# Which engine makes the lo parts of the decoded weights: GpSimd or VectorE

## The chip, the cores and the metric

The kernel runs on one core of one Trainium2 chip. The metric is the device time of one execution in microseconds (us), lower is better; several executions are timed and the median is used. One execution is profiled, and the profile and its trace are what is read here. PE is TensorE (PEld its weight loads), DVE VectorE, ACT ScalarE, POOL GpSimd, SP the engine that issues all DMAs.

## What is computed

The reference chains three blocks on a batch of 4 with 576 positions and 512 channels (8 heads of 64). Cut to what matters:

```python
out_d  = softmax_attention(q_mean4, k_mean4, v_mean4)         # 144 positions
x      = repeat4(out_d) + local_attention(q, k, v, |i-j|<4)   # per head
gate   = sigmoid(causal_conv5(x, conv_w))
x      = (gate * (x @ w_val)) @ w_out
h      = relu(x.T @ w_tok1) @ w_tok2
u      = x + h.T
return u + relu(u @ w_ch1) @ w_ch2
```

All arrays are float32 for the reference. The kernel gets the weights as the bits of 64-bit floats and has to turn them into float32 itself.

## The kernel before

Every large product is made of three TensorE passes (`mm3`, lines 214 to 218): each operand is held as a hi part (rounded to the type fp32r) and a lo part (what the rounding left), and hi*hi, hi*lo and lo*hi are added up.

**Decoding a weight.** `decode` (lines 126 to 151) takes a piece of at most 128 x 256 weights. SP loads the 64-bit words into a tile with the tag `w64` (three buffers). DVE puts the bits together in three steps, lines 135, 136 and 138, into a tile `wa` (three buffers). Then `split` (lines 141 to 143) makes hi on ACT (line 142) and lo on POOL (line 143). A `wa` buffer comes free when its lo is made, so the first step (L135) of the piece three places later waits for that lo.

There are 75 such pieces: 8 of `w_val` (tiles val_hi, val_lo), 8 of `w_out` (out_hi, out_lo), 5 of `w_tok1` (tok_hi, tok_lo), 6 of `w_tok2` (tok_hl), 24 of `w_ch1` (w_hl) and 24 of `w_ch2` (ch). The `w_ch1` tiles are also stored to DRAM as soon as both lo parts are there (line 187, on SP's queue) for use with the later batches.

**Stages.** First (up to about 80 us) the attention of batch 0 runs with the decoding of `w_val` and `w_out` and of the first pieces of `w_tok1`; PE has little to do and is kept going by matmuls on zeros (`busy`, L108). Then a mix of generators runs: `p1(b)` (val product, out product, token products) and `c1(b)` (first channel product) on PE in an order written out by hand (`manual_schedule`), with the attention of batches 1 to 3 and the decoding set between them. The last stage is `c2`, the second channel product.

**Order on the other engines.** DVE, ACT, POOL and SP work in order, each through its own list. A planner makes the lists by priority and by its own estimate of when inputs are ready; nothing is re-ordered while the kernel runs. From the second stage on, `split` is put off until the next piece is decoded (`pending`, `flush`), and its ACT instruction is put behind the ACT copy that empties the latest PE product (`behind_pace`, `paced`).

**What else DVE and POOL do.** DVE makes the convolution (`gate_sb`, L388 and L393), the maxima and reciprocals of the softmax (L251, L261), the sum of the two attentions (`x_f`, L383), `y` (L509) and lo parts that come from PSUM (`x_hl` L533, `r_hl` L574). POOL makes the products by the reciprocal (`e_l`, `e_d`, L262), the sums of v (`v_sb` L291, `vd` L292) and the lo parts of activations (L471).

Of the kernel before, what the change touches and what calls it, by code (L numbers as in the profile page):

```python
# [9 lines left out]
F32 = mybir.dt.float32  # L10
# [5 lines left out]
ALU = mybir.AluOpType  # L16
# [58 lines left out]
def kernel(ctx, tc, qk, vw, v4, w_val, conv_w, w_out, w_tok1, w_tok2, w_ch1, w_ch2, out):  # L75
    nc = tc.nc
# [5 lines left out]
    def T(p, shape, dt, tag, bufs, name=None):  # L82
        return p.tile(shape, dt, tag=tag, bufs=bufs, name=name or tag)
# [37 lines left out]
    def flush():  # L121
        while pending:
            with behind_pace():
                pending.pop(0)()

    def decode(src, n, rows, hi, lo, full=None, shape=None, keep=0):
        x = T(sb, [128, n, 2], I32, "w64", NWD, name="w64")[0:rows]
        a = T(sb, [128, n], I32, "wa", NWD, name="wa")[0:rows]
        if shape is None:
            nc.sync.dma_start(out=x, in_=src.bitcast(I32).rearrange("p (n t) -> p n t", t=2))  # L130
        else:
            nc.sync.dma_start(out=x.rearrange("p (k n) t -> p k n t", k=shape[0]),
                              in_=src.bitcast(I32).rearrange("p k (n t) -> p k n t", t=2))
        low, high = x[:, :, 0], x[:, :, 1]
        nc.vector.tensor_scalar(a, high, 3, 0x3FFFFFF8, ALU.logical_shift_left, ALU.bitwise_and)  # L135
        nc.vector.scalar_tensor_tensor(out=a, in0=high, scalar=-0x40000000, in1=a,  # L136
                                       op0=ALU.bitwise_and, op1=ALU.bitwise_or)
        nc.vector.scalar_tensor_tensor(out=a if full is None else full.bitcast(I32), in0=low, scalar=29, in1=a,
                                       op0=ALU.logical_shift_right, op1=ALU.bitwise_or)

        def split():
            nc.scalar.activation(out=hi, in_=a.bitcast(F32), func=AF.Copy)
            nc.gpsimd.tensor_tensor(out=lo, in0=a.bitcast(F32), in1=hi.bitcast(F32), op=ALU.subtract)

        if full is None:
            if paced[0]:
                if not keep:
                    flush()
                pending.append(split)
            else:  # L150
                split()

    def load_w(key, pieces, tag, bufs, parts=None):

        for j, group in enumerate(pieces):
            n = group[0][1].shape[1]
            hi, lo = parts or [T(sb, [128, len(group), n], F32R, tag, bufs, name=f"{key}{j}_{p}") for p in ("hi", "lo")]
            for i, (rows, src) in enumerate(group):
                for c in range(0, n, WB):
                    e = min(n, c + WB)  # L160
                    decode(src[:, c:e], e - c, rows, hi[0:rows, i, c:e], lo[0:rows, i, c:e])
                wt[key].append((hi[:, i, :], lo[:, i, :]))
                yield
# [16 lines left out]
    def ch1_new(f):  # L180

        t = T(sb, [128, 2, DM], F32R, "w1", NW1R, name="w1_hl")
        src = w_ch1[:, f * 128:f * 128 + 128].rearrange("(k p) c -> p k c", p=128)
        for c in range(0, KC, 2):
            decode(src[:, c:c + 2], 256, 128, *[t[:, i, c * 128:c * 128 + 256] for i in range(2)], shape=(2, 128),
                   keep=c)
        pending.append(lambda: nc.sync.dma_start(out=w1_dr[:, f], in_=t.bitcast(F32)))
        return t
# [6 lines left out]
    def ch2_new():  # L195

        slots = [("wt1", 2)] * 2 + [("w2", NW)] * 8 + [("wt2", 1)]
        f = 0
        for tag, bufs in slots:
            if tag == "w2":  # L200
                pairs = [[T(sb, [128, 1, DM], F32R, tag, bufs, name=f"ch2_{f}_{p}")[:, 0] for p in range(2)]]
            else:
                n = 1 if tag == "wt1" else 2
                t = T(sb, [128, n, 2, DM], F32R, tag, bufs, name=f"ch2_{f}")
                pairs = [[t[:, i, p] for p in range(2)] for i in range(n)]
            for hl in pairs:
                wt["ch2", f] = hl
                for c in range(0, DM, 256):
                    decode(w_ch2[f * 128:f * 128 + 128, c:c + 256], 256, 128, *[t[:, c:c + 256] for t in hl])
                    yield  # L210
                f += 1
        flush()
# [485 lines left out]
    a = [attention(b) for b in range(B)]  # L698
# [7 lines left out]
    side += [(a[b], NA, *A_AT[b]) for b in range(1, B)]  # L706
    last = c2()
    side += [(ch2_new(), 24, *W2_AT), (last, 1, C2_AT, C2_AT + 1)]
    with tc.manual_schedule(engines={mybir.EngineType.PE}):
        mix(first_products(), side)  # L710
# [44 lines left out]
```

## Time and profile before

| | us |
|---|---|
| median of three runs | 664.81 (663.02 to 667.72) |
| the profiled execution, its own time | 669.0 |
| span of the profiled execution, first to last instruction | 667.2 |

| engine | busy us in the span | share |
|---|---|---|
| PE | 626.9 | 94% |
| DVE | 335.7 | 50% |
| ACT | 300.5 | 45% |
| POOL | 209.2 | 31% |

How to read the views: "busy" counts the time in which an engine executes; an instruction's duration includes time in which it is held up at its operands. "Idle before" an instruction is the time in which its engine did nothing, with the instruction that ended the idleness behind an arrow. Times of single instructions are from the start of the span. PEclk is the TensorE clock that was granted, as a share of full speed.

### The profile page before, as it was taken

What the parts mean: (1) busy time and instruction counts of PE and PEld (TensorE: products, weight loads), DVE (VectorE), ACT (ScalarE), POOL (GpSimd) and SP (SyncE); (2) the same over time, 40 slices, a digit from 0 to 9 for tenths busy, and PEclk for the clock granted to TensorE, in tenths of its full rate; (3) what the DMA queues carried; (4) which work ended last, traced back from release to release, by engine and by line L of the source; (5) the groups of instructions that cost most, each with busy time, mean ns of one, the idle gap of its engine ahead of it and who ended that gap; (6) DMA issues with size and microseconds to landing.
All of it is one profiled execution on the core that took longest, in us unless ns stands there. A gap on an engine that the chain in (4) does not pass through costs nothing.

```text
span 667.2 us, 12820 instructions
## 1 busy us (share of the span) xinstructions
PE 626.9 (94%) x4911; PEld 534.6 (80%) x4911; DVE 335.7 (50%) x630; ACT 300.5 (45%) x1032; POOL 209.2 (31%) x242
## 2 busy tenths in 40 slices
PE   8898698888889999999999999999998999999997
PEld 4344487776778988999898999999897888888887
DVE  3679947788795476443343434106626242423232
ACT  1766546564557645637655635324433222222221
POOL 5564613448446432623331323304523000000000
PEclk8899797888989999999999999999998999999999
DMA  7653202565776346784332486566998345454221
GB/s 251 217 160 102 74 21 73 155 209 160 247 231 175 100 165 172 225 244 143 93 87 70 135 240 208 163 196 198 298 299 277 94 139 179 141 175 126 80 69 42
DMA packets 53900, 107.23 MB, mean 161 GB/s; under 512 B 5776, under 2 KB 21392, under 8 KB 53840
## 3 DMA queue, kind: packets, MB, share of 16 engines
q1 hardware_dynamic: 53840, 106.42, 51.8%
q8 instruction: 38, 0.62, 0.4%
q14 instruction: 22, 0.18, 0.1%
HBM read 76.52 MB, written 29.88 MB: 159 GB/s over the span
## 4 chain that ended last, share of the span: by engine, by line
PE 71%; DVE 12%; ACT 6%; DMA 5%; issue 2%; POOL 2%; SPq 1%; DVEq 0%; ACTq 0%; POOLq 0%
PE p_o L216 7%; PE p_o L217 7%; PE p_o L218 7%; PE g_ps L216 6%; PE g_ps L217 6%; PE g_ps L218 6%; DMA w<-in_w_ch_dram 3%; PE sc_l L348 3%; DVE wa L135 3%; DVE wa L136 2%; PE p_x L216 2%; DVE gate_sb L393 2%; PE p_val L217 2%; PE p_val L218 2%; PE p_x L217 2%
## 5 line engine op out<-in xcount | busy, mean ns | idle before, releaser
L216 PE MATMUL g_ps<-u_hl,w_hl 128*128 128x288 f32 x384 | 118.2, 308 | 0.3 <-DVE x_hl L533 0.3
L217 PE MATMUL g_ps<-u_hl,w_hl 128*128 128x288 f32 x384 | 115.5, 301 | 2.5 <-POOL u_hl L471 2.3
L218 PE MATMUL g_ps<-u_hl,w_hl 128*128 128x288 f32 x384 | 114.5, 298 | 0.0
L216 PE MATMUL p_o<-g_hl,ch 128*128 128x512 f32 (+1 forms) x240 | 89.5, 373 | 1.7 <-ACT r_sb L617 1.7
L217 PE MATMUL p_o<-g_hl,ch 128*128 128x512 f32 (+1 forms) x240 | 89.0, 371 | 0.0
L218 PE MATMUL p_o<-g_hl,ch 128*128 128x512 f32 (+1 forms) x240 | 89.0, 371 | 0.0
L471 DVE TENSOR_TENSOR g_hl<-r_back,g_hl 128x512 fp32r<-128x512 f32 (+1 forms) x60 | 38.1, 639 | 92.8 <-ACT g_hl L470 91.2
L470 ACT ACTIVATE g_hl<-r_back 128x512 fp32r<-128x512 f32 (+1 forms) x60 | 35.2, 589 | 108.8 <-PE p_o L218 106.4
L217 PEld LDWEIGHTS g_ps<-u_hl,w_hl 128*128 128x128 f32 x384 | 73.6, 192 | 4.1 <-POOL u_hl L471 4.1
L216 PEld LDWEIGHTS g_ps<-u_hl,w_hl 128*128 128x128 f32 x384 | 73.3, 191 | 4.2 <-issue 2.1
L218 PEld LDWEIGHTS g_ps<-u_hl,w_hl 128*128 128x128 f32 x384 | 73.6, 192 | 0.0
L617 ACT ACTIVATE r_sb<-g_ps 128x288 f32<-128x288 f32 x96 | 38.8, 407 | 61.4 <-PE g_ps L218 52.5
L393 DVE SCALAR_TENSOR_TENSOR gate_sb<-x_f,cw,gate_sb 128x575 f32<-128x575 f32 (+5 forms) x68 | 63.4, 938 | 1.4 <-ACT gate_sb L390 0.5
L216 PEld LDWEIGHTS p_o<-g_hl,ch 128*128 128x128 f32 x240 | 45.6, 190 | 10.1 <-ACT r_sb L617 2.4
L135 DVE TENSOR_SCALAR wa<-w 128x256 int32<-128x256 int32 (+2 forms) x76 | 33.8, 452 | 39.3 <-DMA w<-in_w_ch_dram 21.8
L217 PEld LDWEIGHTS p_o<-g_hl,ch 128*128 128x128 f32 x240 | 45.7, 190 | 7.8
L218 PEld LDWEIGHTS p_o<-g_hl,ch 128*128 128x128 f32 x240 | 45.6, 190 | 7.9
L257 ACT ACTIVATE e_l<-sc_l,mx 128x64 f32<-128x64 f32 x160 | 48.0, 331 | 0.6
L216 PE MATMUL p_val<-x_hl,val_hi 128*128 128x288 f32 x128 | 40.5, 316 | 3.8 <-DVE y L509 2.6
L471 POOL TENSOR_TENSOR x_hl<-x_f,x_hl 128x288 fp32r<-128x288 f32 x32 | 28.1, 889 | 49.4 <-ACT x_hl L470 49.2
L216 PE MATMUL p_x<-y_hl,out_hi 128*128 128x288 f32 x128 | 40.3, 315 | 2.5 <-ACT u_sb L522 1.7
L136 DVE SCALAR_TENSOR_TENSOR wa<-w,wa 128x256 int32<-128x256 int32 (+2 forms) x76 | 41.6, 556 | 1.3
(108 smaller groups left out, 1343.9 us busy)
## 6 DMA issues: line engine op xcount, KB each, us to landing
w_hl<-w_dr SPq DMA_DIRECT2D x36, 512.0 KB
r_dr<-r_sb SPq DMA_DIRECT2D x48, 288.0 KB
w<-in_w_ch_dram SPq DMA_DIRECT2D x48, 256.0 KB
r_back<-r_dr SPq DMA_DIRECT2D x48, 256.0 KB
qk_sb<-in_qk_dram SPq DMA_DIRECT2D x16, 589.0 KB
w_dr<-w_hl SPq DMA_DIRECT2D x12, 512.0 KB
v_sb<-in_vw_dram SPq DMA_DIRECT2D x16, 320.0 KB
v_sb<-in_v_dram SPq DMA_DIRECT2D x16, 288.0 KB
```

Of the source, the lines that this page charges most:

```text
L135: nc.vector.tensor_scalar(a, high, 3, 0x3FFFFFF8, ALU.logical_shift_left, ALU.bitwise_and)
L136: nc.vector.scalar_tensor_tensor(out=a, in0=high, scalar=-0x40000000, in1=a, op0=ALU.bitwise_and, op1=ALU.bitwise_or)
L216: nc.tensor.matmul(out_ap, lhsT=lh, rhs=rh, start=first, stop=False)
L217: nc.tensor.matmul(out_ap, lhsT=lh, rhs=rl, start=False, stop=False)
L218: nc.tensor.matmul(out_ap, lhsT=ll, rhs=rh, start=False, stop=last)
L257: nc.scalar.activation(out=e[:, o, :], in_=p[:, c, :], func=AF.Exp, scale=scale, bias=mx[:, o:o + 1], accum_out=sm[:, o:o + 1])
L348: nc.tensor.matmul(p[r0:r0 + 64, c, :], lhsT=qk[r0:r0 + 64, 0, 3 + o:3 + o + WIN], rhs=qk[r0:r0 + 64, 1, o:o + WIN], start=False, stop=(c ...
L393: nc.vector.scalar_tensor_tensor(out=g[:, t0:s1], in0=x[:, t0 - sh:s1 - sh], scalar=cw[:, hp, k:k + 1], in1=g[:, t0:s1], op0=ALU.mult, op1 ...
L470: nc.scalar.activation(out=hi_ap, in_=src_ap, func=AF.Copy)
L471: lo_eng.tensor_tensor(out=lo_ap, in0=src_ap, in1=hi_ap.bitcast(F32), op=ALU.subtract)
L617: paced[0] = nc.scalar.activation(out=r[:, hv(hs)], in_=p[:, 0:HS], func=AF.Relu)
```

## The change

`decode` gets a parameter for the engine that makes the lo part. Its default is DVE; only the 24 pieces of `w_ch2` keep POOL. So 51 subtractions (8 + 8 + 5 + 6 + 24) go from POOL's list to DVE's. Nothing else differs.

```diff
-    def decode(src, n, rows, hi, lo, full=None, shape=None, keep=0):
+    def decode(src, n, rows, hi, lo, full=None, shape=None, keep=0, lo_eng=nc.vector):
...
         def split():
             nc.scalar.activation(out=hi, in_=a.bitcast(F32), func=AF.Copy)
-            nc.gpsimd.tensor_tensor(out=lo, in0=a.bitcast(F32), in1=hi.bitcast(F32), op=ALU.subtract)
+            lo_eng.tensor_tensor(out=lo, in0=a.bitcast(F32), in1=hi.bitcast(F32), op=ALU.subtract)
...
-                    decode(w_ch2[f * 128:f * 128 + 128, c:c + 256], 256, 128, *[t[:, c:c + 256] for t in hl])
+                    decode(w_ch2[f * 128:f * 128 + 128, c:c + 256], 256, 128, *[t[:, c:c + 256] for t in hl],
+                           lo_eng=nc.gpsimd)
```

## Rows read from the trace of the kernel before

**Rows 1.** Busy time by stage: PE, PEld, DVE, ACT, POOL (instructions), granted clock, DMA share, GB/s.

```profile
0.00:80.00 80.00, 68.99 (x556) 34.68 (x556) 56.54 (x113) 44.96 (x191) 46.45 (x57) 0.91 0.54 168
80.00:260.00 180.00, 159.76 (x1466) 141.18 (x1467) 124.21 (x241) 99.99 (x389) 82.77 (x90) 0.91 0.49 154
260.00:667.20 407.20, 398.18 (x2891) 358.73 (x2889) 154.91 (x278) 155.56 (x454) 79.98 (x95) 0.99 0.54 163
```

**Rows 2.** Longest waits of PE: instruction, who ended it, us, times, longest.

```profile
PE o_d L329 <- DVE x_f L383: 3.2, 1, 3.2
PE pt_d L315 <- DVE x_f L383: 3.0, 1, 3.0
...
PE p_h L216 <- DVE r_hl L574: 2.5, 1, 2.5
```

**Rows 3.** Busy time in stretches with DVE in the chain, columns as in rows 1.

```profile
60.00:80.00 20.00, 15.01 (x150) 8.91 (x148) 18.85 (x31) 12.51 (x31) 13.36 (x13) 0.83 0.38 111
...
133.00:145.00 12.00, 9.50 (x89) 7.17 (x88) 11.97 (x25) 7.57 (x28) 7.90 (x9) 0.96 0.53 181
173.00:181.00 8.00, 5.05 (x75) 4.50 (x74) 7.15 (x12) 2.30 (x9) 5.72 (x6) 1.00 0.75 252
```

**Rows 4.** POOL's busy time in line 143 alone, by stage and stretch (instructions).

```profile
0.00:80.00 80.00, 15.12 (x18) 0.91 0.54 168
80.00:260.00 180.00, 26.45 (x33) 0.91 0.49 154
...
60.00:80.00 20.00, 5.70 (x6) 0.83 0.38 111
...
133.00:145.00 12.00, 5.76 (x7) 0.96 0.53 181
173.00:181.00 8.00, 3.14 (x4) 1.00 0.75 252
```

**Rows 5.** DVE groups by shape: busy us, mean ns of one, idle before.

```profile
L471 DVE TENSOR_TENSOR g_hl<-r_back,g_hl 128x256 fp32r<-128x256 f32 x12 | 5.0, 424 | 12.0 <-ACT g_hl L470 12.0
...
L136 DVE SCALAR_TENSOR_TENSOR wa<-w,wa 128x256 int32<-128x256 int32 x51 | 31.3, 623 | 0.7
L138 DVE SCALAR_TENSOR_TENSOR wa<-w,wa 128x256 int32<-128x256 int32 x51 | 26.5, 526 | 0.7
```

**Rows 6.** DVE in order of time: start, us, instruction, idle before.

```profile
173.93 1.33 DVE L135 TENSOR_SCALAR wa<-w 128x256 int32<-128x256 int32 x1 [0.51 <-POOL w_hl L143]
175.30 0.85 DVE L136 SCALAR_TENSOR_TENSOR wa<-w,wa 128x256 int32<-128x256 int32 x1
176.18 0.85 DVE L138 SCALAR_TENSOR_TENSOR wa<-w,wa 128x256 int32<-128x256 int32 x1
176.96 0.28 DVE L135 TENSOR_SCALAR wa<-w 128x256 int32<-128x256 int32 x1
177.28 0.43 DVE L136 SCALAR_TENSOR_TENSOR wa<-w,wa 128x256 int32<-128x256 int32 x1
177.74 0.83 DVE L138 SCALAR_TENSOR_TENSOR wa<-w,wa 128x256 int32<-128x256 int32 x1
...
188.95 0.42 DVE L138 SCALAR_TENSOR_TENSOR wa<-w,wa 128x256 int32<-128x256 int32 x1
189.29 0.29 DVE L135 TENSOR_SCALAR wa<-w 128x256 int32<-128x256 int32 x1
```

**Rows 7.** POOL in order of time, the same stretch.

```profile
173.15 0.74 POOL L143 TENSOR_TENSOR w_hl<-wa,w_hl 128x256 fp32r<-128x256 f32 x1 [3.00 <-ACT w_hl L142]
173.86 1.26 POOL L262 TENSOR_TENSOR e_l<-e_l,sm 128x640 f32<-128x640 f32 x1
175.07 1.68 POOL L143 TENSOR_TENSOR w_hl<-wa,w_hl 128x256 fp32r<-128x256 f32 x2
177.56 0.72 POOL L143 TENSOR_TENSOR w_hl<-wa,w_hl 128x256 fp32r<-128x256 f32 x1 [0.81 <-ACT w_hl L142]
```

**Rows 8.** DVE's waits for line 143 between 60 and 250 us.

```profile
DVE wa L135 <- POOL w_hl L143: 3.4, 2, 2.9
...
DVE wa L135 <- POOL out_lo L143: 1.1, 1, 1.1
DVE wa L135 <- POOL tok_lo L143: 0.8, 2, 0.5
```

**Rows 9.** A late tok_lo: POOL's row, then DVE's row of that time.

```profile
100.95 0.74 POOL L143 TENSOR_TENSOR tok_lo<-wa,tok_hi 128x256 fp32r<-128x256 f32 x1 [7.97 <-ACT tok_hi L142]
...
95.98 0.82 DVE L251 TENSOR_REDUCE mx<-sc_d 72x2 f32<-72x288 f32 x2 [4.42 <-PE sc_d L302]
```

**Rows 10.** A stretch behind the wait for pt_d, columns as in rows 1.

```profile
180.00:195.00 15.00, 14.73 (x127) 13.74 (x128) 14.03 (x25) 6.61 (x19) 6.04 (x7) 0.77 0.60 193
```

## The prediction

> **What bounds the kernel.** I read the busy times by stage first [rows 1]. After 260 us PE works 398.2 of 407.2 us, and no instruction that moves runs there, so that stage should not change. All 51 of them lie before 260 us: 18 up to 80 us and 33 from there to 260 us, 15.1 + 26.5 = 41.6 us of POOL [rows 4]. In the first 260 us PE has 11.0 + 20.2 = 31.2 us without work, though in the first stage much of its work is only matmuls on zeros. A gain has to come out of these 31 us; a loss can come from anything that makes PE wait longer.
>
> The waits of PE come second [rows 2]. Three of the longest end with a DVE instruction: 3.2 us before o_d (at 69 us), 2.5 us before p_h (144 us), 3.0 us before pt_d (180 us). I then took the busy times of the stretches that lead up to these waits [rows 3]: DVE works 18.85 of 20, 11.97 of 12 and 7.15 of 8 us. So here DVE sets the pace, and POOL (13.4, 7.9 and 5.7 us) does not. The change puts work on the engine that is full. In the rest of the first 260 us DVE has gaps: it works 180.8 us in all, 38.0 of them in these three stretches' 40 us, which leaves 142.8 us of work in 220 us.
>
> Third, the order of time shows what DVE's work is made of when it is full [rows 6, 7]. At 188.95 us an L138 takes 0.42 us and the next instruction starts 0.34 us after it; at 177.28 us an L136 takes 0.43 us. But with an instruction of POOL at work beside it, the same L136 and L138 take 0.85 us, and an L135 of 0.28 us takes 1.33 us while POOL makes e_l in 1.26 us. DVE is not only full of its own work: it is held up by POOL's.
>
> **The change part by part.** Per lo, DVE gets one subtraction of two SBUF inputs.
>
> *Its own price.* The same operation, type and shape is on DVE already, as the lo of g_hl: 424 ns mean over 12 [rows 5], against 0.72 to 0.74 us on POOL [rows 7]. On a full DVE the step to the next instruction counts, 0.34 us [rows 6]. All 51 come to 21.6 us of busy time at 0.424 (three are smaller, so a little less). The three full stretches hold 6 + 7 + 4 = 17 of them [rows 4]: 17 x 0.34 = 5.8 us added.
>
> *What DVE gets back.* Between 175 and 178.6 us three decode steps are held up beside lo's of POOL: 0.85 - 0.43, 0.85 - 0.42 and 0.83 - 0.42, together 1.26 us, and 4 lo's lie in this stretch: 0.31 us per lo [rows 4, 6, 7]. The other way to reckon is by the averages of all pieces: L136 takes 623 ns against 430, L138 526 against 420, so 0.30 us per piece [rows 5, 6]; line 143 is 41.6 of POOL's 129.2 us before 260 us, 32%, so 0.10 us per lo [rows 1, 4]. That average lacks the L135 and the convolutions and mixes in times when DVE had room. Between 0.10 and 0.31 I take 0.25, nearer to the row of a full stretch: 17 x 0.25 = 4.3 us back.
>
> *New collisions.* The moved lo meets what POOL still has to do. L136 and L138 lose 0.15 us on average beside a POOL that is busy 129.2 of 260 us; 68% of that POOL work stays, so 0.10 us per lo, 17 x 0.10 = 1.7 us. The bounds are nothing, if it falls into POOL's gaps, and 0.19 us, L136's whole loss.
>
> The Trainium skill, page "SBUF — State Buffer", section "Who interferes with whom", has it that VectorE and GpSimd share one port pair under an exclusive lock, and that a VectorE instruction with two SBUF inputs contends with a GpSimd instruction that reads SBUF. The 0.85 and the 1.33 us agree with it. By that rule alone the two engines' work adds up in a full stretch, which is the first rival below; it also says that the moved subtraction is itself a holder and a victim of the lock.
>
> *Waits.* L135 waited for line 143 five times between 60 and 250 us, 5.3 us in all [rows 8]. A wa buffer is still freed by the lo, and the lo still waits for ACT's hi, so four of these waits only shrink by the shorter lo, 0.74 - 0.42 = 0.32 us each, 1.3 us. The fifth (out_lo, 1.1 us) goes wholly if POOL's e_l was the reason; I count it. Together 2.4 us back; of these 1.1 (out_lo) and about 0.3 (the L135 at 173.93) lie in the full stretches, 1.4 us.
>
> *POOL.* It loses 41.6 us of work, and so e_l, vd and the other lo's can start earlier. PE's longest waits [rows 2] are not for these: gain taken as nothing; the bound is the lo's own 0.74 us where a POOL product that PE needs stands right behind one.
>
> *ACT and SP.* No instruction is added there. The stores of w_ch1 (L187) wait for the lo and come 0.32 us earlier when it does; three links of the chain go through a lo outside the full stretches (the tok_lo at 100.95 is one [rows 9]). I count 3 x 0.32 = 1.0 us back, the least certain term; it is nothing if PE has other work.
>
> **The sum.** In the full stretches DVE gets 5.8 - 4.3 + 1.7 - 1.4 = +1.8 us, all of it taken as passed on to PE's waits. Less 1.0 us: +0.8 us. In the other stretches DVE's gaps take the 34 remaining lo's; without that cover 34 x 0.42 = 14.3 us would come on top, but DVE is idle for 77 us there. The profiled execution took 669.0 us (span 667.2), above all three timed runs; against it the sum is 669.8 us. Moved to the median, 664.8 + 0.8 = 665.6 us.
>
> **Bounds.** Best: nothing collides anew and 0.31 us come back, 17 x (0.34 - 0.31) - 1.4 - 1.0 = -1.9 us, so 662.9; further down lies only the first rival. Worst without a new stall: nothing comes back and each lo costs 0.424 + 0.193, 17 x 0.617 = +10.5 us, so 675.3. The forecast's own range is 660 to 671.
>
> **Rivals.**
>
> *Faster: POOL's time and DVE's add up.* If in a full stretch every lo on POOL held up DVE for its whole 0.74 us, each one moved saves 0.74 - 0.34 = 0.40 us: 17 x 0.40 = 6.8, and with the 1.0 us of the links 657.0 us. The clock could add to it: in the 15 us from 180 us on, behind the 3.0 us wait for pt_d, the granted clock is 0.77 [rows 10], part of the time at 1.2 instead of 2.4 GHz, which costs up to 0.23 x 15 = 3.4 us of work at full clock. Were that wait to go with what it does to the clock, 657.0 - 3.4 = 653.6 us. For it: the 0.85 us rows. Against it: while POOL made two lo's from 175.07 to 176.75 (1.68 us) [rows 7], DVE lost 0.85 us, half of it. The exclusive lock of the Trainium skill's page "SBUF — State Buffer" ("Who interferes with whom") is this rival taken strictly.
>
> *Slower: a lo stands in DVE's list before its hi is there.* On POOL a waiting lo delays little; on DVE everything behind it waits. The place: the tok_lo at 100.95 us came after POOL had waited 7.97 us for ACT's tok_hi [rows 9]. If the planner puts it on DVE ahead of the mx at 95.98 us, DVE stands until 100.9 us, 4.9 us, and behind it wait the softmax of the next head and the y that PE needs. A second place is the lo at 173.15 us, for which POOL waited 3.0 us [rows 7]. Both together give 665.6 + 7.9 = 673.5 us. It decides from the point at which the planner's time for ACT's hi is some 5 us earlier than the chip's. Against it: lists of ACT and DVE come out of one plan, and the L135 that needs the buffer of a late lo is on DVE already and waited for it 2.9 us at most and 1.1 us on average [rows 8].
>
> *Slower: DVE is simply too full.* Nothing comes back because POOL's other work moves into the gaps: the worst bound above, 675.3 us. For it: 11.97 of 12 us [rows 3]. Against it: the 1.26 us that go back in one stretch.
>
> **Chances.** The forecast 0.52; POOL's time comes off 0.23; a lo blocks DVE 0.17; too full 0.08. About 1% (6.6 us) is what a measurement of this kernel tells from no change. The first rival ends beyond -1%; with it 0.01 of the forecast's tail makes faster 0.24. The two slower ones are 0.25, and 0.51 are left for within 1%. Range: 656 to 676 us takes in 657.0, 673.5 and 675.3, and leaves out the clock's extra gain and several blocks at once, together 0.2.
>
> **What would show it.** Right: line 143 on DVE at about 0.42 us alone, 0.5 to 0.55 us mean; L136 and L138 means down from 623 and 526 towards 550 and 480 ns; DVE busy up by some 8 to 14 us before 260 us; POOL down by 41.6 us; o_d, p_h and pt_d waits within 1 us of now; from 260 us on the same times. The first rival: L136 and L138 near 430 ns and these three waits shorter by 1 us and more, the clock after 180 us higher. The second: DVE idle before line 143 for ACT's hi by several us, with PE waits for mx, y or x_f behind it. What makes the forecast wrong most easily is the list: with 51 more instructions the planner can order DVE's others differently.

## The result, and the profile after

The changed kernel takes 657.81 us (median; 657.43 to 659.81 over 4 runs). The kernel before, timed beside it, took 664.66 us. The ratio is 0.9887 with a 95% interval of 0.9853 to 0.9920: faster by 1.1%, which is 7.5 us of 665 (the two medians differ by 6.9). The time lies inside the predicted range of 656 to 676 us, but below the forecast's own 660 to 671, and the forecast (665.6 us, within 1%) was wrong; the first rival's 657.0 us is close. The profiled execution of after took 657.43 us (span 655.6).

Busy time by stage, kernel after, columns as in [rows 1]:

```profile
0.00:80.00 80.00, 64.68 (x557) 33.64 (x560) 62.56 (x132) 45.12 (x191) 34.78 (x40) 0.96 0.52 168
80.00:260.00 180.00, 165.12 (x1573) 145.66 (x1572) 131.25 (x285) 104.82 (x406) 60.99 (x59) 0.94 0.50 159
260.00:640.00 380.00, 375.27 (x2691) 337.44 (x2692) 146.17 (x257) 148.18 (x431) 77.68 (x92) 1.00 0.55 170
```

and the last of these stretches in the kernel before:

```profile
260.00:640.00 380.00, 375.75 (x2726) 337.47 (x2725) 146.27 (x259) 151.30 (x444) 79.98 (x95) 1.00 0.56 170
```

Against [rows 1], DVE works 13.1 us more before 260 us (62.56 + 131.25 against 56.54 + 124.21) and POOL 33.5 us less. PE gets 5.4 us more work into the stretch from 80 to 260 us, and its granted clock there rises from 0.91 to 0.94. From 260 us on PE is as full as before. The first channel product's end shows how much was gained ahead of it: the first matmul of p_o starts at 500.8 us instead of 510.1, the first p_h at 137.6 instead of 144.3, but the first p_val at 76.2 instead of 77.3. (These 9 us are of two single executions; that of before ran above its median, as the prediction noted.)

DVE's groups before 260 us (busy us, mean ns, idle before), L135 in the kernel before, then the kernel after:

```profile
L135 DVE TENSOR_SCALAR wa<-w 128x256 int32<-128x256 int32 x51 | 24.7, 494 | 15.6 <-DMA w<-in_w_val_dram 8.7 <-POOL w_hl L143 3.4 <-DMA w<-in_w_ch_dram 1.4
```

```profile
L138 DVE SCALAR_TENSOR_TENSOR wa<-w,wa 128x256 int32<-128x256 int32 x51 | 24.4, 485 | 0.3
L136 DVE SCALAR_TENSOR_TENSOR wa<-w,wa 128x256 int32<-128x256 int32 x51 | 23.4, 472 | 0.3
L135 DVE TENSOR_SCALAR wa<-w 128x256 int32<-128x256 int32 x51 | 15.9, 326 | 9.0 <-DMA w<-in_w_val_dram 7.6 <-DMA w<-in_w_ch_dram 1.3
L143 DVE TENSOR_TENSOR w_hl<-wa,w_hl 128x256 fp32r<-128x256 f32 x24 | 14.6, 642 | 0.2
...
L143 DVE TENSOR_TENSOR val_lo<-wa,val_hi 128x256 fp32r<-128x256 f32 x8 | 5.9, 750 | 0.7 <-ACT val_hi L142 0.7
...
L143 DVE TENSOR_TENSOR out_lo<-wa,out_hi 128x256 fp32r<-128x256 f32 x8 | 4.2, 550 | 0.7 <-ACT out_hi L142 0.7
```

The 51 lo's take 28.7 us of DVE, 0.56 us each (those of tok_lo and tok_hl, 4.0 us together, are not shown). L136 and L138 fall from 623 and 526 ns [rows 5] to 472 and 485, and L135 from 494 to 326. The three steps of a piece thus take 1.28 us instead of 1.64: 0.36 us back per piece. That is less than the lo's own 0.56 us, so DVE's busy time grows, and the kernel is faster all the same.

PE's waits before 260 us, kernel after (line numbers from 209 on are higher by one):

```profile
PE o_l L378 <- ACT pts_l L367: 6.3, 3, 4.4
...
PE p_val L217 <- DVE y L510: 2.9, 2, 2.7
PE o_d L330 <- ACT pts_d L319: 2.6, 5, 1.0
...
PE p_h L217 <- DVE r_hl L575: 1.7, 1, 1.7
...
PE pt_d L316 <- DVE x_f L384: 0.8, 1, 0.8
```

Of the three waits in [rows 2], the 3.2 us before o_d is gone, pt_d's fell from 3.0 to 0.8 and p_h's from 2.5 to 1.7. The wait before p_val stayed (2.6 us before, 2.7 after). The longest new one, 4.4 us before an o_l, lies at 57 us in the stage with the zeros.

### The profile page after: what moved, and what is told of

The parts are those of the page before. It is cut to its first block, busy times and chain, and to the rows that moved or that the text cites. A ratio compares the mean times of both kernels' runs of the same rounds, so it can differ in the third digit from the quotient of the medians.

```text
span 655.6 us, 12806 instructions
## 1 busy us (share of the span) xinstructions
PE 616.1 (94%) x4909; PEld 527.6 (80%) x4911; DVE 343.7 (52%) x681; ACT 299.8 (46%) x1032; POOL 173.4 (26%) x191
## 4 chain that ended last, share of the span: by engine, by line
PE 66%; DVE 13%; DMA 8%; ACT 6%; POOL 3%; issue 2%; SPq 1%; DVEq 0%; ACTq 0%; POOLq 0%
PE p_o L217 7%; PE p_o L219 7%; PE p_o L218 7%; DMA w<-in_w_ch_dram 5%; PE g_ps L217 5%; PE g_ps L218 5%; PE g_ps L219 5%; DVE gate_sb L394 3%; PE sc_l L349 3%; ACT e_l L258 3%; PE p_x L217 2%; PE p_val L217 2%; PE p_val L219 2%; PE p_val L218 2%; DVE wa L136 2%
## 5 line engine op out<-in xcount | busy, mean ns | idle before, releaser
L217 PE MATMUL g_ps<-u_hl,w_hl 128*128 128x288 f32 x384 | 117.0, 305 | 0.0
L218 PE MATMUL g_ps<-u_hl,w_hl 128*128 128x288 f32 x384 | 114.1, 297 | 1.2 <-POOL u_hl L472 0.9
L219 PE MATMUL g_ps<-u_hl,w_hl 128*128 128x288 f32 x384 | 113.3, 295 | 0.0
L217 PEld LDWEIGHTS g_ps<-u_hl,w_hl 128*128 128x128 f32 x384 | 72.4, 189 | 3.2 <-issue 1.9
L218 PEld LDWEIGHTS g_ps<-u_hl,w_hl 128*128 128x128 f32 x384 | 72.6, 189 | 2.4 <-POOL u_hl L472 2.4
L219 PEld LDWEIGHTS g_ps<-u_hl,w_hl 128*128 128x128 f32 x384 | 72.5, 189 | 0.0
L394 DVE SCALAR_TENSOR_TENSOR gate_sb<-x_f,cw,gate_sb 128x575 f32<-128x575 f32 (+3 forms) x68 | 64.9, 960 | 0.8
L217 PE MATMUL p_val<-x_hl,val_hi 128*128 128x288 f32 x128 | 41.3, 323 | 4.2 <-DVE y L510 2.9
L135 DVE TENSOR_SCALAR wa<-w 128x256 int32<-128x256 int32 (+2 forms) x76 | 24.4, 334 | 32.2 <-DMA w<-in_w_ch_dram 20.6
L218 PE MATMUL p_val<-x_hl,val_hi 128*128 128x288 f32 x128 | 39.5, 309 | 1.1 <-POOL x_hl L472 1.1
```

The source lines that it names most:

```text
L217: nc.tensor.matmul(out_ap, lhsT=lh, rhs=rh, start=first, stop=False)
L218: nc.tensor.matmul(out_ap, lhsT=lh, rhs=rl, start=False, stop=False)
L219: nc.tensor.matmul(out_ap, lhsT=ll, rhs=rh, start=False, stop=last)
L394: nc.vector.scalar_tensor_tensor(out=g[:, t0:s1], in0=x[:, t0 - sh:s1 - sh], scalar=cw[:, hp, k:k + 1], in1=g[:, t0:s1], op0=ALU.mult, op1 ...
```

## Experiments

Five theories were to be told apart; the number in brackets is the one that the expectations use. **Reads** (theory 1): a subtraction on POOL reads two SBUF tiles, and while it does, DVE's steps are held up; the lo's on POOL cost the kernel more by this than they cost on DVE. **POOL's list** (4): products such as e_l stand behind lo's. **Buffers** (3): L135 no longer waits for a `wa` buffer. **Lists** (2): the planner happened to order the engines better. **Clock** ((a) in f1 and f2): the gain is TensorE's granted clock, and the waits matter only through it. Theory 5, in e9 and e10, is Reads with one price and one return for every lo, wherever it lies.

All results as ratio to the kernel before, and in us at 665 us:

| run | ratio (95%) | us |
|---|---|---|
| the change | 0.9887 (0.9853 to 0.9920) | -7.5 |
| e1: only the 24 w_ch1 lo's on DVE | 0.9948 (0.9927 to 0.9969) | -3.5 |
| e2: only the other 27 | 0.9938 (0.9906 to 0.9969) | -4.1 |
| e9: only the 17 of the full stretches | 0.9914 (0.9884 to 0.9945) | -5.7 |
| e10: only the other 34 | 0.9975 (0.9953 to 0.9997) | -1.7 |
| e4: before, POOL reads 8 of 256 columns | 0.9807 (0.9773 to 0.9840) | -12.8 |
| e3: after, POOL reads again for all 51 | 1.0100 (1.0060 to 1.0140) | +6.6 |
| f3: after, POOL reads again for the 17 | 0.9994 (0.9971 to 1.0017) | -0.4 |
| f4: after, POOL reads again for the 34 | 1.0010 (0.9990 to 1.0030) | +0.7 |
| g1: after, POOL reads again for the first 18 | 0.9966 (0.9936 to 0.9995) | -2.3 |
| g2: after, POOL reads again for the last 33 | 1.0046 (1.0020 to 1.0073) | +3.1 |
| e5: after, POOL as busy, mostly writing | 0.9914 (0.9887 to 0.9942) | -5.7 |
| e6: before, four wa buffers | 0.9998 (0.9976 to 1.0020) | -0.1 |
| e7: before, one more matmul on zeros at the start | 0.9988 (0.9974 to 1.0002) | -0.8 |
| e8: after, one more matmul on zeros at the start | 0.9892 (0.9863 to 0.9921) | -7.2 |
| f1: before, matmuls on zeros added | 0.9988 (0.9966 to 1.0010) | -0.8 |
| f2: after, matmuls on zeros added | 0.9952 (0.9933 to 0.9972) | -3.2 |
| e11: after, x and u lo's of batch 0 on DVE too | 0.9931 (0.9903 to 0.9958) | -4.6 |
| e12: e11 and softmax products on DVE | 0.9879 (0.9838 to 0.9920) | -8.0 |

**Parts of the change, e1 and e2.** e1 moves only the pieces of w_ch1, e2 all but these.

```diff
 # e1
-    def decode(..., lo_eng=nc.vector):
+    def decode(..., lo_eng=nc.gpsimd):
...
-                   keep=c)
+                   keep=c, lo_eng=nc.vector)
 # e2: the default stays nc.vector
+                   keep=c, lo_eng=nc.gpsimd)
```

> Only the 24 lo's of w_ch1 go to DVE; the 27 of w_val, w_out, w_tok1 and w_tok2 stay on POOL. Theory 1 (POOL's lo's hold up DVE, so each one taken off POOL shortens the full stretches of DVE): the stage up to about 130 us is as before, the gain of the stretch from 133 to 200 us is there, so about half of the 7 us: 660 to 662 us. Theory 2 (the gain comes from the first stage, where the planner put DVE's and PE's instructions in another order): 664 to 665 us.

> The 27 lo's of w_val, w_out, w_tok1 and w_tok2 go to DVE, the 24 of w_ch1 stay on POOL. Theory 1: the other half, 660 to 662 us, with p_val starting about 1 us earlier. Theory 2 (new order in the first stage): all of the gain, 657 to 659 us. If the parts do not add up to 7 us, neither is right in this form.

They came to -3.5 and -4.1 us, together -7.6 against -7.5 for the whole. In this split the gain goes with the number of lo's (24 and 27), 0.15 us each, as theory 1 had it.

**POOL's reads put back or taken away, e3 and e4.** e3 is the changed kernel, and POOL subtracts hi from itself, full size, into a scratch tile. In program order its lists on PE, DVE, ACT and SP are those of after, instruction by instruction; only POOL's is longer. e4 is the kernel before with the subtraction on 8 of 256 columns and zeros in the rest: most of the lo part is left out, and no lo is made on DVE.

```diff
 # e3
+            if lo_eng is nc.vector:
+                s = T(sb, [128, 256], F32R, "scr", 1)[0:rows, 0:n]
+                nc.gpsimd.tensor_tensor(out=s, in0=hi.bitcast(F32), in1=hi.bitcast(F32), op=ALU.subtract)
 # e4
+            e = cut or n      # cut is 8 for the 51 pieces, 0 for w_ch2
+            if cut:
+                nc.gpsimd.memset(lo.bitcast(F32)[:, 8:n], 0.0)
+            nc.gpsimd.tensor_tensor(out=lo[:, 0:e], in0=a.bitcast(F32)[:, 0:e], in1=hi.bitcast(F32)[:, 0:e], op=ALU.subtract)
```

> The changed kernel, and for each of the 51 pieces POOL also makes a subtraction of the same size (hi minus hi, into a tile that nobody reads). POOL's work is that of the kernel before again, but nobody waits for it and it does not hold a wa buffer. Theory 1 (the collisions with POOL's reads set the time): the gain goes and more, since DVE has its own 51 on top: 665 to 670 us, with L135 and L136 back at about 490 and 620 ns. Theory 3 (the gain is the shorter way from hi to lo, and wa coming free earlier): stays at 657 to 660 us.

> The kernel before, but the 51 lo's are cut on POOL to 8 of 256 columns, and POOL fills the rest with zeros (this part of the computation is left out). DVE gets nothing. Theory 1: this has the gain of the change without its price on DVE, so at least as fast as the changed kernel, 652 to 658 us, with L135 and L136 at or below the changed kernel's 326 and 472 ns. Theory 2 (order): no bound between the two, anything from 655 to 666 us.

POOL's 51 reads cost 14.1 us (e3 against after) or 12.8 us (before against e4): 0.25 to 0.28 us each. The 51 lo's on DVE cost 5.3 us (after against e4) or 6.6 us (e3 against before): 0.10 to 0.13 us each. The difference is the gain. Each of these four is a difference of two ratios with an interval of 2 to 3.5 us either way. DVE's groups in e3:

```profile
L138 DVE SCALAR_TENSOR_TENSOR wa<-w,wa 128x256 int32<-128x256 int32 x51 | 27.6, 548 | 0.3
L136 DVE SCALAR_TENSOR_TENSOR wa<-w,wa 128x256 int32<-128x256 int32 x51 | 26.9, 540 | 0.3
L135 DVE TENSOR_SCALAR wa<-w 128x256 int32<-128x256 int32 x51 | 18.7, 384 | 7.8 <-DMA w<-in_w_val_dram 7.8
...
L143 DVE TENSOR_TENSOR out_lo<-wa,out_hi 128x256 fp32r<-128x256 f32 x8 | 6.3, 816 | 0.7 <-ACT out_hi L142 0.7
```

Every step is longer than in after (485, 472, 326 and 550 ns), with the same instructions in the same order. The three steps of 51 pieces are longer by 9.6 us, the lo's by 4.7 us (33.4 against 28.7), and the kernel by 14.1 us. The same steps in e4:

```profile
L136 DVE SCALAR_TENSOR_TENSOR wa<-w,wa 128x256 int32<-128x256 int32 x51 | 27.3, 547 | 0.6
L138 DVE SCALAR_TENSOR_TENSOR wa<-w,wa 128x256 int32<-128x256 int32 x51 | 23.9, 476 | 0.6
L135 DVE TENSOR_SCALAR wa<-w 128x256 int32<-128x256 int32 x51 | 18.8, 376 | 12.6 <-DMA w<-in_w_val_dram 7.5 <-POOL w_hl L146 3.3 <-POOL out_lo L146 0.6
```

Here one sign missed: L136 and L135 were expected at or below after's 472 and 326 ns and took 547 and 376. Against the kernel before, the three groups are shorter by 12.5 us (70.0 against 82.5), and the kernel by 12.8 us. So in both runs the kernel's time moved by about as much as POOL's reads moved DVE's steps. The 28.7 us of lo's in DVE's list cost it only 5.3 to 6.6 us. Why the one passes through to the end and the other mostly does not is not shown.

**Reading or only being busy, e5.** After, and for each of the 51 POOL reads 8 columns and then fills the scratch tile twice.

```diff
+                nc.gpsimd.tensor_tensor(out=s[0:rows, 0:8], in0=hi.bitcast(F32)[:, 0:8], in1=hi.bitcast(F32)[:, 0:8], ...)
+                nc.gpsimd.memset(s[0:rows], 0.0)
+                nc.gpsimd.memset(s[0:rows, 0:128], 0.0)
```

> The changed kernel, and for each of the 51 pieces POOL subtracts 8 columns (hi minus hi) and then fills 256 and 128 columns with zeros, in a tile that nobody reads: POOL is as long at work per piece as in the run before this one, about 0.75 us, but reads little. Theory 1 (what costs is that POOL's reads collide with DVE): most of the 14 us of that run go away, 658 to 663 us. Theory 4 (what costs is POOL's own list: e_l, e_d and the other lo's stand behind the extra work): the 14 us stay, 668 to 674 us.

Busy time by stage in e5, then in e3:

```profile
0.00:80.00 80.00, 65.85 (x554) 34.42 (x556) 59.77 (x132) 44.97 (x191) 49.50 (x93) 0.94 0.52 166
80.00:260.00 180.00, 160.78 (x1520) 141.98 (x1521) 131.66 (x281) 103.48 (x401) 88.99 (x157) 0.95 0.50 159
```

```profile
0.00:80.00 80.00, 65.39 (x540) 33.16 (x541) 60.95 (x121) 41.46 (x182) 46.00 (x56) 0.87 0.51 161
80.00:260.00 180.00, 157.55 (x1472) 140.00 (x1470) 136.61 (x280) 102.77 (x396) 84.14 (x90) 0.92 0.48 154
```

POOL is busier in e5 (138.5 us before 260 us) than in e3 (130.1 us), with the same lists elsewhere, and e5 costs 1.8 us over after where e3 costs 14.1. DVE's steps stay near after's (472 and 326 ns):

```profile
L136 DVE SCALAR_TENSOR_TENSOR wa<-w,wa 128x256 int32<-128x256 int32 x51 | 24.5, 492 | 0.3
L135 DVE TENSOR_SCALAR wa<-w 128x256 int32<-128x256 int32 x51 | 17.2, 351 | 8.5 <-DMA w<-in_w_val_dram 7.5 <-DMA w<-in_w_ch_dram 0.9
```

The theory of POOL's list falls: POOL's time as such is worth little (the 1.8 us lie inside the intervals); its reading is what costs. The Trainium skill, page "SBUF — State Buffer", section "Who interferes with whom", says that a VectorE instruction with two SBUF inputs contends with a GpSimd instruction that reads SBUF and not with one that only writes it; these two runs agree, 14.1 against 1.8 us.

One rival is left: a fill takes 0.32 or 0.21 us and a read in e3 0.78 us (w_hl), so that the length of one POOL instruction counts, and not its reading, is not excluded.

**The buffers and the lists, e6, e7, e8.** e6 gives the kernel before a fourth `wa` buffer. e7 and e8 change the number of zero matmuls at the start, in before and in after, which was expected to make the planner write other lists.

```diff
 # e6
-        a = T(sb, [128, n], I32, "wa", NWD, name="wa")[0:rows]
+        a = T(sb, [128, n], I32, "wa", NWD + 1, name="wa")[0:rows]
 # e7, e8
-NW0, NW1 = 8, 3
+NW0, NW1 = 9, 3
```

> The kernel before with four instead of three wa buffers, so that a first decode step no longer waits for the lo of the piece three places earlier. Theory 3 (wa comes free earlier when DVE makes lo): some of the 7 us, 660 to 663 us. Theory 1: the 5.3 us of waits for line 143 were mostly covered or wait for hi anyway: within 2 us of the kernel before, 664 to 667 us.

> The kernel before with nine instead of eight matmuls on zeros at its start. The work is the same but for 0.2 us of PE time in the shadow of the first loads; the planner's lists of the first stage come out differently on all engines. Theory 2 (the gain is a matter of how the lists fall): a difference from the kernel before of several us, in either direction. Theory 1: within 2 us, 664 to 667 us.

> The changed kernel with nine instead of eight matmuls on zeros at its start. Theory 2: several us away from the changed kernel's 658 us. Theory 1: 656 to 660 us, and some 7 us below the kernel before with nine.

e6 gives -0.1 us, but it does not decide the theory of the buffers: L135's waits for line 143 between 60 and 250 us fell only from 5.3 to 4.1 us.

```profile
DVE wa L135 <- POOL w_hl L143: 2.5, 2, 1.9
DVE wa L135 <- POOL tok_lo L143: 0.8, 2, 0.5
DVE wa L135 <- POOL out_lo L143: 0.6, 1, 0.6
DVE wa L135 <- POOL tok_hl L143: 0.2, 1, 0.2
```

e3 and e4 decide it. In e3 L135 waits for no lo on POOL, and the gain is gone; in e4 it still waits 3.9 us (its row above), and the kernel is 12.8 us faster. The gain does not hang on these waits.

e7 and e8 missed their purpose: in their traces DVE, ACT, POOL and SP run the instructions of before and of after in the same order. They show that the change is worth the same again, 6.4 us (-0.8 and -7.2). The theory of the lists falls by other runs: e6 has other lists than before on DVE, ACT and POOL and stays at -0.1 us; e3, with after's lists, loses the gain; e4, with lists close to before's, gains 12.8 us.

**Where the reads cost, e9, e10, f3, f4, g1, g2.** e9 and e10 split the change into the 17 lo's of the prediction's full stretches and the rest. f3 and f4 are e3 for the same 17 and 34; g1 and g2 are e3 for the pieces decoded before and after 80 us. f3, f4, g1 and g2 have after's lists on the other engines.

```diff
+    full_stretch = set(range(12, 18)) | {26} | set(range(27, 33)) | set(range(35, 39))
 # e9 (e10: not in)
+            lo_eng = nc.vector if count[0] in full_stretch else nc.gpsimd
 # f3 (f4: not in; g1, g2: the first 18, the others): e3's subtraction only for these
+        again = full is None and lo_eng is nc.vector and count[0] in full_stretch
```

> Only those 17 lo's go to DVE that lie in the three stretches in which DVE was full (out's last four, tok1's first two, tok2's last, and w_ch1's 1st to 6th and 9th to 12th); the other 34 stay on POOL. The prediction's account (only these 17 matter, the other 34 are covered): the whole effect of the change, 657 to 659 us. Theory 5 (each lo off POOL is worth the same 0.24 us and costs 0.1 us on DVE, wherever it lies before 260 us): a third of the 7 us, 662.5 to 664 us.

> The other way round: these 17 lo's stay on POOL, and the 34 that lie where DVE had gaps go to DVE. The prediction's account: no effect, 664 to 666.5 us. Theory 5: two thirds of the 7 us, 660 to 662 us.

> The changed kernel; POOL makes the extra subtraction that nobody waits for (hi minus hi, full size) for the 17 pieces of the full stretches only. If collisions cost where DVE is full: most of the 14.5 us that all 51 cost, 666 to 670 us. If they cost alike everywhere: a third, 662 to 664 us.

> The same for the other 34 pieces. If collisions cost where DVE is full: 658 to 662 us. If alike everywhere: two thirds of the 14.5 us, 667 to 669 us.

> The changed kernel, its lists for TensorE, VectorE, ScalarE and the DMAs left as they are; GpSimd makes one more subtraction (hi - hi, into a scratch tile) for the first 18 pieces alone, which are decoded before 80 us. Their place is the attention of batch 0, where TensorE is kept busy with zeros. If VectorE sets the pace all through this stage, the reads put back cost about half of the 12 to 14.5 us that they cost for all 51: 5 to 7 us more than the changed kernel, 663 to 665 us. If only the 6 of the stretch from 60 to 80 us count, as the prediction had it, 6 x 0.44 = 2.6 us, 660.5 us. If what is lost on zeros does not reach the end, no change from 658 us.

> The same for the other 33 pieces, decoded after 80 us, among them 11 of the 17 of the full stretches. If the first stage carries half, the other half is here: 5 to 8 us more than the changed kernel, 663 to 666 us. If the full stretches alone count, 11 x 0.44 = 4.8 us, 663 us. If nearly everything comes from the first stage, 658 to 660 us.

Moving the 17 alone brings three quarters of the gain, the 34 a quarter. But the reads put back cost 7.1 us for the 17 and 8.2 us for the 34, and 5.2 us for the first 18 and 10.6 us for the last 33: 0.24 to 0.42 us each. The sums, 15.3 and 15.8 us, are near e3's 14.1, inside their intervals. So the reads of the 34 do cost. Moving these 34 brings little because they cost almost as much on DVE: 6.4 us, from f4 against e9 (+0.7 and -5.7). For the 17 the same reckoning (f3 against e10) gives 1.3 us. Each of these two is a difference between kernels with other lists and intervals of about 2 us, so only their order of size is safe. Theory 5 is wrong for the net gain, which is 0.34 us per lo for the 17 and 0.05 for the 34, and the prediction's account is wrong for the reads. How much of g2's 10.6 us are its reads is not certain: in its profiled execution the first p_val starts at 80.5 us, 4.3 us later than in after, though no read is put back ahead of it (see the last section).

**The clock, f1 and f2.** Before and after with 8 matmuls on zeros in front of the first p_val and 10 in front of the first p_h.

```diff
+    def warm(p, n):
+        for _ in range(n):
+            nc.tensor.matmul(p, lhsT=idle[:, 0:128], rhs=idle, start=True, stop=True)
...
+                if b + hs + c == 0:
+                    warm(p, 8)
```

> The kernel before, with 8 matmuls on zeros in front of the first p_val product and 10 in front of the first p_h product (1.7 and 2.1 us at full clock), written to the bank that the product then starts over. PE waits there for 2 to 3 us for its operands anyway. If the clock that falls behind such waits is a large part of the price (a): 2 to 4 us less than the kernel before, and a higher mean clock. If the collisions' price is DVE's delay alone (b): the same time, or up to 2 us more.

> The changed kernel with the same 18 matmuls on zeros. Its waits at these two places are shorter (1.7 us before p_h), so under (a) the gain is smaller than on the kernel before: 0 to 2 us less than the changed kernel. Under (b): 0 to 2 us more.

Busy time from 80 to 260 us in f1:

```profile
80.00:260.00 180.00, 158.91 (x1517) 138.62 (x1517) 127.76 (x249) 102.47 (x393) 82.02 (x89) 0.95 0.48 156
```

The granted clock is 0.95 here, more than after's 0.94, and over the whole timed runs its mean rose from 0.9705 to 0.9762. The time did not follow: -0.8 us, with no change inside the interval, and f2 lost 4.3 us of after's gain. A higher clock bought with zeros brings nothing, so the clock is not shown to be the cause. But the added matmuls take PE's time themselves: 1.7 + 2.1 = 3.8 us by f1's expectation, and the clock's rise of 0.0057 over 665 us is 3.8 us as well. Gain and price may have cancelled, so this theory is not refuted either.

**More of the same, e11 and e12.** e11 moves the lo's of x and u of batch 0 to DVE as well, e12 also the softmax products of batches 0 and 1.

```diff
-                hi_lo(xf[b][k][:, hv(hs)], x[0][:, k], x[1][:, k], nc.gpsimd)
+                hi_lo(xf[b][k][:, hv(hs)], x[0][:, k], x[1][:, k], nc.gpsimd if b else nc.vector)
...
-        nc.gpsimd.tensor_tensor(out=e, in0=e, in1=bc(sm, w), op=ALU.mult)
+        eng.tensor_tensor(out=e, in0=e, in1=bc(sm, w), op=ALU.mult)
```

> The changed kernel, and for batch 0 the lo's of the activations x (8) and u (8) go from POOL to DVE as well. Theory 1 with the prices measured so far (0.24 us back per 0.74 us of POOL's reading, 0.1 us for each subtraction on DVE): 16 x 0.16 = 2.6 us less than the changed kernel, 654.5 to 656.5 us. If DVE is at its limit before the first products: 658 us or more.

> As the run before it, and the softmax products e_l and e_d of batches 0 and 1 (16 of 1.15 to 1.27 us on POOL) go to DVE too. Theory 1 by the same prices per us of reading: some 3 us less again, 651 to 654 us. The rival (DVE is full in the first stage, and the product stands between the softmax and the transposes of PE): 656 us or more.

-4.6 and -8.0 us: neither is better than the change itself by more than its interval, and both miss what theory 1 gave by its prices. e11 was to be 2.6 us faster than the change and came out 2.9 us slower. That DVE has by now what it can take is a likely reason; it was not tested.

## Why the prediction was wrong, step by step

**The step that failed** is the sum of the full stretches [rows 3], 5.8 - 4.3 + 1.7 - 1.4 = +1.8 us for their 17 lo's. e9 moves just these 17, and the kernel became 5.7 us faster. Two terms of the sum were mis-sized.

- *The price on DVE*, 5.8 + 1.7 = 7.5 us, rests on the step that on a full DVE the time of every moved lo is passed on to PE. Measured are 1.3 us for the 17 (f3 against e10), and all 51 together cost only 5.3 to 6.6 us.
- *What DVE gets back*, 4.3 us, measured 7.1 us in f3, 0.42 us per lo where 0.25 was taken. Over all 51 it is 0.25 to 0.28 us each, 12.8 to 14.1 us. The interval of 7.1 is nearly 3 us either way, so the price is the surer of the two.

The other 34 lo's were put at nothing, because DVE is idle for 77 us there. Their net came out near that, -1.7 us (e10), but by luck: their reads cost 8.2 us (f4) and they themselves 6.4 us on DVE. So DVE's idle time is no cover for either. A likely reason is that a collision lengthens whichever step is running, and where the next link of a chain waits for that step, idle time behind it does not help; that is argued and not measured.

**DVE's own price in the trace.** In the full stretch that ends with p_h's wait, DVE's rows from x_f to r_hl show how little the lo's cost. Before:

```profile
129.21 0.83 DVE L383 TENSOR_TENSOR x_f<-o_l,x_f 128x290 f32<-128x290 f32 x2 [3.19 <-PE o_l L377]
...
138.52 1.65 DVE L136 SCALAR_TENSOR_TENSOR wa<-w,wa 128x256 int32<-128x256 int32 x2
140.09 0.75 DVE L138 SCALAR_TENSOR_TENSOR wa<-w,wa 128x256 int32<-128x256 int32 x2
...
143.56 1.28 DVE L574 SCALAR_TENSOR_TENSOR r_hl<-r_ps,r_hl 128x512 fp32r<-128x512 f32 x2
```

After:

```profile
122.47 0.76 DVE L384 TENSOR_TENSOR x_f<-o_l,x_f 128x290 f32<-128x290 f32 x2
...
130.06 0.42 DVE L143 TENSOR_TENSOR w_hl<-wa,w_hl 128x256 fp32r<-128x256 f32 x1
...
131.45 1.37 DVE L143 TENSOR_TENSOR w_hl<-wa,w_hl 128x256 fp32r<-128x256 f32 x1
...
134.08 0.74 DVE L136 SCALAR_TENSOR_TENSOR wa<-w,wa 128x256 int32<-128x256 int32 x2
134.75 0.74 DVE L138 SCALAR_TENSOR_TENSOR wa<-w,wa 128x256 int32<-128x256 int32 x2
135.42 1.08 DVE L143 TENSOR_TENSOR w_hl<-wa,w_hl 128x256 fp32r<-128x256 f32 x3
...
136.89 1.27 DVE L575 SCALAR_TENSOR_TENSOR r_hl<-r_ps,r_hl 128x512 fp32r<-128x512 f32 x2
```

From x_f's start to r_hl's it is 14.35 us before and 14.42 us after, although five lo's of w_ch1 and a small one of tok_hl (0.21 us) now stand between. Free of POOL, two L136 take 0.74 us and two L138 0.74 us (1.65 and 0.75 before), and three lo's 1.08 us, 0.36 each. One lo of 1.37 us met POOL's e_d of 1.24 us at 131.30 and took about as long. So in this pair price and return cancel in this stretch, and what is gained was gained ahead of x_f, which starts 6.7 us earlier. (In e7 and e8, which have the same two lists, x_f starts at 127.37 and 123.12 us, 4.3 us apart.)

**POOL's share of the blame.** The low bound of the return, 0.10 us per lo, put 32% of the loss of DVE's steps down to line 143, by its share of POOL's busy time. In fact 0.19 of the 0.30 us that L136 and L138 lost per piece came back, two thirds, and another 0.17 us on L135, which this average had left out. The lo's follow the decode steps closely in time, so a likely reason is that they meet them more often than POOL's other work does; that was not measured by itself. The upper bound of 0.31, from one stretch [rows 6], was the better reading. The prediction's sentence on two SBUF inputs does not cover the 1.33 us that it names beside the 0.85, since L135 has one such input; that L135 loses time beside POOL is what the rows show.

**The waits for `wa`** were counted at 1.4 us in the full stretches. In the kernel after, L135 waits for no lo any more, but e6, which was to show what that is worth, kept most of these waits, so this term is open. The **1.0 us of chain links** has no run of its own and is open too.

**The first rival** (POOL's time and DVE's add up, 657.0 us) comes closest. Its 6.8 us for the 17 lo's measured 5.7 us in e9; the 34 add 1.7. Its number is right partly by luck: it took back 0.74 us per lo and paid 0.34, where f3 gives 0.42 back and so a price of about 0.08. Its signs are half there: L136 and L138 went to 472 and 485 ns, not to 430; two of the three waits shrank by more than 1 us. The clock is there as well. From pt_d to the next p_val, the stretch of [rows 10], the same 121 matmuls stand in both kernels; before, then after:

```profile
180.20:194.30 14.10, 14.03 (x121) 13.04 (x122) 13.13 (x23) 6.12 (x17) 6.04 (x7) 0.76 0.57 186
```

```profile
170.10:181.00 10.90, 10.88 (x121) 10.28 (x122) 10.05 (x23) 5.08 (x15) 3.10 (x3) 1.00 0.85 273
```

PE is busy throughout in both, and the stretch is 3.2 us shorter at the full clock; the rival's bound was 3.4 us. Such a pair varies: in e7 and e8 the stretch takes 12.5 and 10.9 us.

**The second rival** (a lo waits for its hi and blocks DVE) fell. All waits of the moved lo's for their hi before 260 us, kernel after:

```profile
DVE out_lo L143 <- ACT out_hi L142: 0.7, 1, 0.7
DVE val_lo L143 <- ACT val_hi L142: 0.7, 2, 0.4
DVE tok_hl L143 <- ACT tok_hl L142: 0.5, 1, 0.5
```

The late tok_lo [rows 9] starts at 97.62 us on DVE, behind a reciprocal and without a wait, and takes 0.39 us. **The third** (DVE too full, nothing back) fell too, with its condition half met: DVE is full (16.0 of the 16 us from 60 to 76 us), and busier by 13 us, inside the forecast's 8 to 14.

**What held:** the same times from 260 us on; a lo of 0.41 us alone and 0.56 mean (0.42, 0.50 to 0.55 foreseen). POOL lost 35.8 us over the whole span (209.2 to 173.4) instead of 41.6: its other operations became longer, before 260 us vd from 791 to 953 ns and v_sb from 1381 to 1451. That POOL is now the one held up there is likely, not shown.

**What stays open:** how the time splits between DVE's steps and TensorE's clock. Over the timed runs, the share of the clock not granted, times the span, is 14.3 us in after and 18.6 to 20.4 us in before. Reads put back into after raise it by 5.0 us (g1), 5.7 (f3), 6.5 (f4), 9.7 (g2) and 11.5 us (e3), about four fifths or more of what they cost. The stretch from pt_d to p_val shows one way. In after, e5 and e8, where pt_d waits 0.8 to 1.0 us for x_f, its 121 matmuls take 10.9 to 11.0 us; in e3, f3, f4, g1 and g2, with the same lists and waits of 2.0 to 3.7 us, 12.3 to 15.3 us. In e3:

```profile
181.70:197.00 15.30, 15.28 (x121) 14.39 (x122) 14.23 (x30) 6.22 (x17) 7.02 (x8) 0.67 0.69 227
```

So part of what a held-up DVE costs comes out as a lower clock on PE's own work. It is not all: e4's share is 14.3 us like after's, and e4 is 5.3 us faster. No run parts the clock from the waits that go with it, and part of the low clock lies on zeros, where it need not cost anything.

## What to carry to other kernels

An operation on POOL that reads SBUF is not free because POOL is idle: here each cost the kernel 0.25 to 0.28 us by holding up DVE, about twice what the same operation cost on DVE itself (0.10 to 0.13 us), although DVE was the busier engine. Look for DVE instructions of one form with two lengths (0.42 and 0.85 us), ask which POOL instruction lies beside the long ones, and reckon the return over all of them, not only where DVE is full. One run in which POOL reads almost nothing (e4 here) then tells, before anything is moved, how much there is to win; it does not tell what the operations will cost on the other engine, and a full engine's busy time did not tell it either (7.5 us reckoned, 1.3 measured for the 17).

## What the runs showed of the hardware that was not expected

The same work of PE ran at two speeds in kernels with the same lists. The first p_val products with what lies between them, in f3 and in after:

```profile
79.90:95.60 15.70, 11.26 (x62) 10.79 (x61) 10.63 (x26) 6.22 (x16) 4.82 (x3) 0.78 0.14 39
```

```profile
76.20:87.00 10.80, 8.96 (x62) 8.24 (x61) 10.11 (x24) 5.86 (x16) 2.90 (x3) 1.00 0.21 57
```

The 62 matmuls span 15.70 us at a granted clock of 0.78, partly at 1.2 GHz, and 10.80 us at 1.00, all at 2.4 GHz. PE is busy for 11.26 and 8.96 us of them, so 2.3 of the 4.9 us are its own work at the lower clock and the rest are waits. The first p_val started 3.7 us later in f3 than in after, and this stretch ended 8.6 us later: a delay in a stage of zeros came out larger behind the first real product.

And single executions differ in the same stage. Before 80 us g2 has no instruction that after has not, only a scratch tile more; in its profiled execution

```profile
0.00:80.00 80.00, 68.50 (x544) 34.70 (x545) 57.91 (x123) 42.23 (x184) 31.35 (x38) 0.85 0.52 164
```

the granted clock is 0.85 instead of 0.96, and DVE's instruction at 76 us of after starts 4.4 us later. One profile says little about a few us before 80 us; the verdicts above rest on the timed runs.
